# Twenty operand sums per second layer moved from VectorE to GpSimd, one unit ahead

## The chip, the cores and the metric

One core of one Trainium2 chip. The metric is the device time of one execution in microseconds (us). The engines are named as the profile names them: PE is TensorE's matmul, PEld its weight load, DVE is VectorE, ACT ScalarE, POOL GpSimd, SP the queue that issues the DMAs.

## The reference

```python
scores = scale * q @ k.T - log(S)          # 8 batches, 12 heads, 448 tokens, 64 per head
attn   = sigmoid(scores);  x = attn @ v    # x: 3584 tokens by 768
h = x @ w_in                               # 768 -> 2048
g = s * relu(h)**2 + b
out = g @ w_out                            # 2048 -> 768
```

All arrays are fp32, and products are taken nearly in fp32: an operand is split into a high part (its rounding to the format that TensorE multiplies) and a low part (the rest), and each product is three matmuls, high by high, high by low, low by high.

## The kernel before, in words

**Attention** (to 250 us of the span) writes x, transposed, to DRAM, while the weights are converted and their sums are made. **Tokens 0 to 511** pass through the feed-forward network in the plain way. The other six blocks of 512 tokens are done in two **threes**, n = 0 and 1, by a fast matrix algorithm with 15 products in place of 18. Each three has a first and a second layer.

In the **first layer** (the loop over L1, line 1080) the 15 products of x with w_in run in chains that add up in PSUM. Their results are combined on VectorE and ScalarE (`results_1`) into tiles G[m, h, p], with m the token block, h the half of the hidden dimension and p one of four parts. Each finished G is squared after its ReLU on VectorE (line 857) and scaled and shifted on ScalarE (line 860).

In the **second layer** (the loop over L2, line 1210) the 15 products come in the order 8, 13, 6, 10, 7, 1, 2, 3, 5, 4, 11, 12, 14, 0, 9, each with its four parts p: 60 **units** j of 12 matmuls. A unit's operand comes either straight from one G, from a G changed in place, or, for the products 6, 10, 7, 1 and 5, from a sum or difference of two G's in a fresh tile `gs_{n}_{i}_{p}`. 5 products by 4 parts are twenty fresh sums per second layer, forty in all.

`prep(j + LEAD)` with LEAD = 3, called behind unit j, makes the operand of the unit three ahead: its source (for the five products the sum, by `new`, line 1025), then its high part on ScalarE (`split_hi`, lines 678 and 680). The same call makes the low part of the unit two ahead on VectorE (`split_lo`, lines 181 and 689), and frees a fresh source. Two products also change G in place there: product 2 subtracts from G[0, 0], product 3 adds G[0, 0] to G[0, 1], which product 5's sums read later.

The order on each engine is the order in which the code is written; nothing reorders it. An engine runs ahead of the others as far as its waits let it. The tiles `gs`, `g_..h`, `g_..l`, `C` and others share 46 slots of one size (`heap`), handed out first freed, first used: a tile waits until the last reader of its slot's earlier tile is done. `results_2` copies the products' PSUM results out on ScalarE (line 1141) or combines them on VectorE with C tiles, and stores these. GpSimd has no work in this kernel beyond four constants at the start.

The weights `wu` come by DMA, one tile per unit, six units ahead.

Of the kernel before, what the change touches and what calls it, by code (L numbers as in the profile page):

```python
# [18 lines left out]
ALU = mybir.AluOpType  # L19
# [75 lines left out]
def sigmoid_attention_relu2_ffn(  # L95
# [10 lines left out]
    nc = tc.nc  # L106
    B, NQ, P, _, _, S = qk.shape
    D = v.shape[5]
    NF, _, DM = w_in.shape
# [67 lines left out]
    def add(o, x, y):  # L177
        nc.vector.tensor_tensor(o, x, y, op=ALU.add)  # L178

    def sub(o, x, y):  # L180
        nc.vector.tensor_tensor(o, x, y, op=ALU.subtract)  # L181
# [44 lines left out]
    def op(o, x, sign, y):  # L226
        (add if sign > 0 else sub)(o, x, y)
# [426 lines left out]
    L2 = [(i, p) for i in ORDER_2 for p in range(NPP)]  # L654
# [11 lines left out]
    def slot(name, r=False):  # L666
        return heap.tile([P, 2, TB], F32R if r else F32, name=name)
# [7 lines left out]
    def split_hi(raw, sign, name):  # L675
        hi = slot(name + "h", True)
        if sign > 0:
            nc.scalar.copy(hi, raw)
        else:
            nc.scalar.activation(hi, raw, AF.Copy, scale=-1.0)  # L680
        return hi

    def split_lo(raw, sign, hi, name, own):

        lo = slot(name + "l", True)
        if sign > 0:
            sub(lo, raw, f32(hi))
        else:
            nc.vector.scalar_tensor_tensor(
                lo, raw, -1.0, f32(hi), op0=ALU.mult, op1=ALU.subtract  # L690
            )
        if own:
            heap.free(raw)
        return lo
# [56 lines left out]
    def activate(f, ph):  # L751
        g = gp.tile([P, 2, TB], F32R, tag="g", name=f"g_{f}")
        r = rt.tile([P, TB], F32, tag="r", name=f"r_{f}")
        nc.scalar.activation(r, ph, AF.Relu)
        nc.scalar.activation(r, r, AF.Square)
        nc.scalar.activation(r, r, AF.Identity, bias=b_sb, scale=s_sb)
        nc.scalar.copy(g[:, 0], r)
        sub(g[:, 1], r, f32(g[:, 0]))
        return g
# [20 lines left out]
    for i, f in enumerate(order):  # L780
# [14 lines left out]
        g = activate(f, ph)  # L795
        if i + 1 < NF:
            w2[i + 1] = base(1, order[i + 1])
        j, stage = divmod(i - LATE_AT, LATE_FOR)
# [152 lines left out]
    for n, blocks in enumerate(threes):  # L951

        G = {}
# [6 lines left out]
        def results_1(i, p, bk):  # L960
# [9 lines left out]
            def final(m, h, neg=False):  # L970
                x = g(m, h)
                if (m, h) == (0, 0):
                    scales.append(lambda: (act_square(x), scale(x)))
                else:
                    later.append(lambda: (square(x, neg), scales.append(lambda: scale(x))))
# [36 lines left out]
            else:  # L1012
                add(g(2, 1), g(2, 1), bk)
                final(2, 1)

        def prep(j):

            if 0 <= j < len(L2):
                i, p = L2[j]
                own = True  # L1020

                def g(m, h):
                    return G[m, h, p]

                def new(x, sign, y):
                    t = slot(f"gs_{n}_{i}_{p}")
                    op(t, x, sign, y)
                    return t

                def drop(m, h):  # L1030
                    heap.free(G.pop((m, h, p)))

                def take(m, h):
                    return G.pop((m, h, p))

                if i in (8, 13, 2, 3):
                    src, own = G[{8: (1, 0), 13: (0, 1), 2: (2, 0), 3: (2, 1)}[i] + (p,)], False
                elif i == 6:
                    src = new(g(0, 1), -1, g(1, 0))
                elif i == 10:  # L1040
                    src = new(g(0, 1), 1, g(1, 1))
                elif i == 7:
                    src = new(g(0, 0), 1, g(1, 0))
                elif i == 1:
                    src = new(g(0, 0), 1, g(0, 1))
                elif i == 5:
                    src = new(g(2, 1), -1, g(0, 1))
                elif i == 4:
                    src = take(0, 1)
                elif i == 12:  # L1050
                    src = take(0, 0)
                elif i == 11:
                    add(g(1, 0), g(1, 0), g(1, 1))
                    src, own = G[1, 0, p], False
                elif i == 14:
                    sub(g(1, 0), g(2, 1), g(1, 0))
                    src, own = G[1, 0, p], False
                elif i == 0:
                    add(g(2, 0), g(2, 0), g(1, 0))
                    src = take(2, 0)  # L1060
                else:
                    sub(g(1, 1), g(2, 1), g(1, 1))
                    src = take(1, 1)
                sign = SECOND[i][1]
                gc[j] = (src, own, split_hi(src, sign, f"g_{n}_{i}_{p}"))
                if i == 2:
                    sub(g(0, 0), g(0, 0), g(2, 0))
                if i == 3:
                    add(g(0, 1), g(0, 1), g(0, 0))
                if i == 0:  # L1070
                    drop(1, 0)
                if i == 9:
                    drop(2, 1)
            j -= 1
            if 0 <= j < len(L2):
                i, p = L2[j]
                src, own, hi = gc[j]
                gc[j] = (hi, split_lo(src, SECOND[i][1], hi, f"g_{n}_{i}_{p}", own))

        for u, (i, p) in enumerate(L1):  # L1080
# [35 lines left out]
            if u >= len(L1) - LEAD:  # L1116
                prep(u - len(L1) + LEAD)
# [92 lines left out]
        for j, (i, p) in enumerate(L2):  # L1210
# [5 lines left out]
            g = gc.pop(j)  # L1216
            end = n + 1 == len(threes) and j + 1 == len(L2)

            for e, tk in LAST if end else [(e, slice(TB)) for e in range(KC)]:
# [11 lines left out]
                if end:  # L1231
                    x = C["t"][:, e, tk]
# [9 lines left out]
            if j in loads:  # L1242
                load_raw(n + 1, *loads[j])
            prep(j + LEAD)
            if later:
                later.popleft()()
# [43 lines left out]
```

## Time and profile before

| | us |
|---|---|
| median of 3 runs | 1038.89 |
| lowest and highest run | 1038.45, 1038.98 |
| the profiled execution, first to last instruction (span) | 1037.2 |
| first layer of three 0, on the chain of matmuls | 163.20 |
| second layer of three 0 | 163.20 |
| first layer of three 1 | 163.20 |
| second layer of three 1 | 163.28 |

The profiled execution's time is given by the page as its span alone; the median of the timed runs lies 1.7 us above it.

How to read the views. A row of the timeline has the start, the duration, the engine, the line, the operation, the tile written and the tiles read, and, in brackets, how long the engine had been idle before and who ended that. Buffer numbers are left out of the names: `g_2l` is the low part for part 2 of whichever product comes at that time, `gs` is a fresh sum, `h` and `o` are PSUM results of the first and the second layer. Line 178 is VectorE's add, line 181 its subtract; both are helpers, so the line alone doesn't tell the place. A row of groups has the count, the busy time and the mean of one, and the idle time before them.

### The profile page before, as it was taken

To read this page: it belongs to the slowest core of one execution; us is meant where nothing else is said; L and a number is where in the kernel's file an instruction comes from. 1 tells how busy PE (TensorE), PEld (TensorE's weight loads), DVE (VectorE), ACT (ScalarE), POOL (GpSimd) and SP (SyncE) were. 2 spreads that over 40 slices of the span, in tenths; PEclk is the share of its full clock that TensorE was granted. 3 is DMA by queue.
4 is the path that set the end of the run, shared out by engine and by line. 5 is a ranking of instruction groups with operands and counts; after the bars stand their busy time and mean duration, and the time that the engine had idled before them with its cause. 6 is when DMAs were issued, how large, how long until landed. Compare 5 with 4: busy or idle time off the path is not lost.

```text
span 1037.2 us, 13906 instructions
## 1 busy us (share of the span) xinstructions
PE 1033.5 (100%) x5290; PEld 780.9 (75%) x5290; DVE 837.3 (81%) x910; ACT 617.0 (59%) x666; POOL 0.2 (0%) x4
## 2 busy tenths in 40 slices
PE   9999999999999999999999999999999999999998
PEld 4545555555888888888888888888888888888887
DVE  5999999995988965898898897796455789888777
ACT  7999999988776755564445344344445335552432
POOL 0000000000000000000000000000000000000000
PEclk9999999999999999999999999999999999999999
DMA  9788989994999999999686676897666666676773
GB/s 334 265 333 340 359 321 393 345 398 190 338 362 366 358 409 410 340 341 322 201 267 190 218 230 219 292 317 249 197 192 194 194 192 196 191 233 212 221 227 119
DMA packets 101569, 287.17 MB, mean 277 GB/s; under 512 B 10240, under 2 KB 20352, under 8 KB 101504
## 3 DMA queue, kind: packets, MB, share of 16 engines
q1 hardware_dynamic: 101216, 285.84, 79.3%
q8 instruction: 42, 0.69, 0.3%
q10 hardware_dynamic: 288, 0.46, 0.1%
q14 instruction: 23, 0.19, 0.0%
HBM read 198.18 MB, written 88.08 MB: 276 GB/s over the span
## 4 chain that ended last, share of the span: by engine, by line
PE 100%; DVE 0%; issue 0%
PE o L1225 31%; PE h L1095 31%; PE pav L454 11%; PE psc L420 9%; PE ph L563 6%; PE po L765 6%; PE psc_l L441 2%; PE pav L463 2%; PE idle L482 0%; PE psc L426 0%; DVE C_t L181 0%
## 5 line engine op out<-in xcount | busy, mean ns | idle before, releaser
L1095 PE MATMUL h<-s_0h,wu 128*128 128x512 f32 x480 | 148.0, 389 | 0.0
L1095 PE MATMUL h<-s_1h,wu 128*128 128x512 f32 x480 | 147.8, 389 | 0.0
L400 ACT ACTIVATE a<-psc,nls 128x896 f32<-128x896 f32 x144 | 132.7, 1008 | 12.9 <-PE psc L420 10.1
L454 PE MATMUL pav<-a,v 128*64 128x448 f32 x576 | 113.8, 543 | 0.0
L1095 PEld LDWEIGHTS h<-s_0h,wu 128*128 128x128 f32 x480 | 90.1, 188 | 18.8
L1095 PEld LDWEIGHTS h<-s_1h,wu 128*128 128x128 f32 x480 | 90.1, 188 | 18.6
L968 ACT COPY G<-h 128x1024 f32<-128x1024 f32 x48 | 48.8, 1017 | 85.4 <-PE h L1095 57.7
L860 ACT ACTIVATE G<-G,b_sb,s_sb 128x1024 f32<-128x1024 f32 x48 | 59.8, 1246 | 61.4 <-DVE G L857 60.7
L1095 PE MATMUL h<-s_0l,wu 128*128 128x512 f32 x240 | 93.4, 389 | 0.0
L1095 PE MATMUL h<-s_1l,wu 128*128 128x512 f32 x240 | 93.4, 389 | 0.0
L454 PEld LDWEIGHTS pav<-a,v 128*64 128x64 f32 x576 | 39.1, 137 | 63.8 <-issue 45.4
L178 DVE TENSOR_TENSOR G<-G,h 128x1024 f32<-128x1024 f32 x40 | 48.8, 1219 | 39.1 <-PE h L1095 38.9
L1225 PE MATMUL o<-g_3h,wu 128*128 128x512 f32 (+1 forms) x244 | 79.0, 385 | 0.0
L1225 PE MATMUL o<-g_1h,wu 128*128 128x512 f32 x240 | 78.8, 389 | 0.0
L1225 PE MATMUL o<-g_2h,wu 128*128 128x512 f32 x240 | 78.8, 389 | 0.0
L1225 PE MATMUL o<-g_0h,wu 128*128 128x512 f32 x240 | 78.8, 389 | 0.0
L765 PE MATMUL po<-g,w 128*128 128x512 f32 x288 | 67.7, 389 | 0.0
L765 PEld LDWEIGHTS po<-g,w 128*128 128x128 f32 x288 | 54.1, 188 | 11.2
L563 PE MATMUL ph<-x0h,w 128*128 128x512 f32 x192 | 61.7, 390 | 0.0
L420 PE MATMUL psc<-qkh 64*128 64x448 f32 x284 | 54.8, 382 | 0.0
L1225 PEld LDWEIGHTS o<-g_3h,wu 128*128 128x128 f32 x244 | 45.6, 188 | 9.2
L1225 PEld LDWEIGHTS o<-g_0h,wu 128*128 128x128 f32 x240 | 45.1, 188 | 9.4
(152 smaller groups left out, 2029.7 us busy)
## 6 DMA issues: line engine op xcount, KB each, us to landing
wu<-wd SPq DMA_DIRECT2D x240, 512.0 KB, 3.8
wd<-t SPq DMA_DIRECT2D x36, 768.0 KB, 8.1
qk<-qk_t SPq DMA_DIRECT2D x23, 896.0 KB, 7.1
st<-w_out SPq DMA_DIRECT2D x16, 768.0 KB, 9.3
st<-w_in SPq DMA_DIRECT2D x16, 768.0 KB, 9.2
wd<-w SPq DMA_DIRECT2D x16, 768.0 KB, 5.9
v<-v_t SPq DMA_DIRECT2D x24, 448.0 KB, 5.4
xd<-xo SPq DMA_DIRECT2D x24, 448.0 KB, 4.4
```

The costliest lines, as they stand in the source:

```text
L178: nc.vector.tensor_tensor(o, x, y, op=ALU.add)
L400: nc.scalar.activation(a, psc[:, :, :S], AF.Sigmoid, bias=nls, scale=SCALE)
L420: nc.tensor.matmul(o[:, j, :S], two[wi][r, i, cols], two[xi][r, i, :S], start=m == 0, stop=m == 2,)
L441: nc.tensor.matmul(psc[half[i], j, :S], x[r, i, 1, 3 * P :], x[r, i, 0, :], start=True, stop=True,)
L454: nc.tensor.matmul(pav[r, i, :S], ld_[1][:, 3 * i + c, j, :], a[i, c][:, j, :], start=c == 0, stop=False,)
L463: nc.tensor.matmul(pav[r, i, :S], ld_[1][half[i], 6, j, :], a[half[i], j, :], start=False, stop=True,)
L563: nc.tensor.matmul(ph, w[:, k, wi, kc * P : (kc + 1) * P], x0[h][xi][:, cc, :], start=m == 0, stop=m == 3 * NCC - 1,)
L765: nc.tensor.matmul(pos[e], w[:, k, wi, kc * P : (kc + 1) * P], g[:, gi, :], start=first and i == 0, stop=last and i == 2,)
L860: nc.scalar.activation(x, x, AF.Identity, bias=b_sb, scale=s_sb)
L968: nc.scalar.copy(g(m, h), bk)
L1095: nc.tensor.matmul(bk[:, j], wt[:, j, wi, c * P : (c + 1) * P], opd[i][xi][:, c, :], start=i == ch[0] and m == 0, stop=m == 3 * KC - 1, sk ...
L1225: nc.tensor.matmul(o, wt[:, f, wi, e * P : (e + 1) * P], g[gi][:, f, tk], start=(end or i == ch[0] and p == 0) and f == 0 and m == 0, stop ...
```

## The change

The five kinds of sum move into a table. `prep(j)` first issues, on GpSimd, the sum for unit j + 1, if that unit is one of the five products, and keeps the tile in `made`; for unit j itself it takes the tile that the call before made. So a sum is issued one unit earlier than before, and on another engine.

```diff
+        NEW = {
+            6: ((0, 1), -1, (1, 0)), 10: ((0, 1), 1, (1, 1)), 7: ((0, 0), 1, (1, 0)),
+            1: ((0, 0), 1, (0, 1)), 5: ((2, 1), -1, (0, 1)),
+        }
+        made = {}
+
         def prep(j):
 
+            if 0 <= j + 1 < len(L2) and L2[j + 1][0] in NEW:
+                i, p = L2[j + 1]
+                x, sign, y = NEW[i]
+                made[j + 1] = slot(f"gs_{n}_{i}_{p}")
+                nc.gpsimd.tensor_tensor(
+                    made[j + 1], G[x + (p,)], G[y + (p,)], op=ALU.add if sign > 0 else ALU.subtract
+                )
...
-                def new(x, sign, y):
-                    t = slot(f"gs_{n}_{i}_{p}")
-                    op(t, x, sign, y)
-                    return t
...
-                elif i == 6:
-                    src = new(g(0, 1), -1, g(1, 0))
...
+                elif i in NEW:
+                    src = made.pop(j)
```

On VectorE, at the turn from product 13 to product 6 of three 0, stood before (gs_6_2 is the fresh sum for product 6, part 2; the number behind it is the buffer's):

```order
L181 TENSOR_TENSOR g_13_1l<-G_011_4114,g_13_1h 128x1024
L181 TENSOR_TENSOR g_13_2l<-G_012_4224,g_13_2h 128x1024
L181 TENSOR_TENSOR gs_6_0_5155<-G_010_4094,G_100_4355 128x1024
L181 TENSOR_TENSOR g_13_3l<-G_013_4243,g_13_3h 128x1024
L181 TENSOR_TENSOR gs_6_1_5175<-G_011_4114,G_101_4377 128x1024
L689 SCALAR_TENSOR_TENSOR g_6_0l<-gs_6_0_5155,g_6_0h 128x1024
L181 TENSOR_TENSOR gs_6_2_5195<-G_012_4224,G_102_4487 128x1024
```

and now, on the same engine:

```order
L181 TENSOR_TENSOR g_13_1l<-G_011_4114,g_13_1h 128x1024
L181 TENSOR_TENSOR g_13_2l<-G_012_4224,g_13_2h 128x1024
L181 TENSOR_TENSOR g_13_3l<-G_013_4243,g_13_3h 128x1024
L689 SCALAR_TENSOR_TENSOR g_6_0l<-gs_6_0_5137,g_6_0h 128x1024
L689 SCALAR_TENSOR_TENSOR g_6_1l<-gs_6_1_5157,g_6_1h 128x1024
L689 SCALAR_TENSOR_TENSOR g_6_2l<-gs_6_2_5177,g_6_2h 128x1024
```

The sums are gone from between the low halves, whose own order is as it was. They are GpSimd's queue now, whose first rows are these (it had no sums before; the first row is the branch at the program's start):

```order
L1286 UNCONDITIONAL_BRANCH
L1028 ISA
L1028 TENSOR_TENSOR gs_6_0_5137<-G_010_4094,G_100_4355 128x1024
L1028 TENSOR_TENSOR gs_6_1_5157<-G_011_4114,G_101_4377 128x1024
L1028 TENSOR_TENSOR gs_6_2_5177<-G_012_4224,G_102_4487 128x1024
L1028 TENSOR_TENSOR gs_6_3_5197<-G_013_4243,G_103_4505 128x1024
L1028 TENSOR_TENSOR gs_10_0_5219<-G_010_4094,G_110_4613 128x1024
```

GpSimd holds nothing but the forty sums, in the order of the units, so each starts when its two G's and its slot are there, whatever VectorE is at.

Later in the same layer, on VectorE, the low halves of product 3 (g_3) with the additions into G[0, 1] between them, before:

```order
L178 TENSOR_TENSOR G_013_4243<-G_013_4243,G_003_3946 128x1024
L689 SCALAR_TENSOR_TENSOR g_3_2l<-G_212_4139,g_3_2h 128x1024
L181 TENSOR_TENSOR gs_5_0_5645<-G_210_4007,G_010_4094 128x1024
L689 SCALAR_TENSOR_TENSOR g_3_3l<-G_213_4167,g_3_3h 128x1024
L181 TENSOR_TENSOR gs_5_1_5665<-G_211_4025,G_011_4114 128x1024
L181 TENSOR_TENSOR g_5_0l<-gs_5_0_5645,g_5_0h 128x1024
```

and now:

```order
L178 TENSOR_TENSOR G_013_4243<-G_013_4243,G_003_3946 128x1024
L689 SCALAR_TENSOR_TENSOR g_3_2l<-G_212_4139,g_3_2h 128x1024
L689 SCALAR_TENSOR_TENSOR g_3_3l<-G_213_4167,g_3_3h 128x1024
L181 TENSOR_TENSOR g_5_0l<-gs_5_0_5626,g_5_0h 128x1024
L181 TENSOR_TENSOR g_5_1l<-gs_5_1_5647,g_5_1h 128x1024
```

Product 5's sums no longer stand behind product 3's low halves; on GpSimd each waits only for the addition into its own G[0, 1, p]. On ScalarE and in SP's queue nothing changes its place.

More of the change, by code (lines that the diff above doesn't have):

```diff
@@ L1037, in prep @@
                     src, own = G[{8: (1, 0), 13: (0, 1), 2: (2, 0), 3: (2, 1)}[i] + (p,)], False
-                elif i == 6:
-                    src = new(g(0, 1), -1, g(1, 0))
[L1040 to L1047, printed above, removed]
+                elif i in NEW:
+                    src = made.pop(j)
                 elif i == 4:
```

## The prediction

> **What bounds the kernel now.** I read the page's busy times first, then the chain that ended last in order of time, then TensorE's waits.
>
> ```profile
> span 1037.2 us, 13906 instructions
> PE 1033.5 (100%) x5290; PEld 780.9 (75%) x5290; DVE 837.3 (81%) x910; ACT 617.0 (59%) x666; POOL 0.2 (0%) x4
> ```
>
> ```profile
> 544.55 163.20 PE o L1225 x720
> 707.75 163.20 PE h L1095 x720
> 870.95 163.28 PE o L1225 x726
> ```
>
> ```profile
> PE idle L482 <- PEq L1280: 0.8, 1, 0.8
> ```
>
> TensorE is busy for the whole span, the chain is matmuls almost throughout, and in all its waits there is one row, 0.8 us at the start. The two second layers take 163.20 us for 720 matmuls each: 226.7 ns per matmul, 2.72 us per unit of 12. So VectorE's relief can't shorten the chain: work taken off an engine that nobody on the chain waits for is worth nothing. What the change can do is make an operand late. The question is how late VectorE's low halves run against the matmul that reads them.
>
> The timeline of TensorE gives the due times, the second layer's first two matmuls on the high and the low tile of product 8, part 0:
>
> ```profile
> 544.39 0.39 PE L1225 MATMUL o<-g_0h,wu 128*128 128x512 f32 x1
> 544.62 0.39 PE L1225 MATMUL o<-g_0l,wu 128*128 128x512 f32 x1
> ```
>
> So the low tile of unit j is due at 544.62 + 2.72 j. The timeline of VectorE around that point:
>
> ```profile
> 522.83 1.22 DVE L181 TENSOR_TENSOR G<-G,h 128x1024 f32<-128x1024 f32 x1 [0.24 <-PE h L1095]
> 524.08 1.22 DVE L857 SCALAR_TENSOR_TENSOR G<-G 128x1024 f32<-128x1024 f32 x1
> 525.55 1.22 DVE L181 TENSOR_TENSOR G<-G,h 128x1024 f32<-128x1024 f32 x1 [0.24 <-PE h L1095]
> 526.80 1.22 DVE L857 SCALAR_TENSOR_TENSOR G<-G 128x1024 f32<-128x1024 f32 x1
> 528.27 1.22 DVE L181 TENSOR_TENSOR G<-G,h 128x1024 f32<-128x1024 f32 x1 [0.24 <-PE h L1095]
> ...
> 539.15 1.22 DVE L181 TENSOR_TENSOR G<-G,h 128x1024 f32<-128x1024 f32 x1 [0.24 <-PE h L1095]
> ...
> 543.69 1.22 DVE L181 TENSOR_TENSOR g_1l<-G,g_1h 128x1024 fp32r<-128x1024 f32 x1
> 544.82 1.22 DVE L857 SCALAR_TENSOR_TENSOR G<-G 128x1024 f32<-128x1024 f32 x1
> 545.96 1.21 DVE L178 TENSOR_TENSOR G<-G,h 128x1024 f32<-128x1024 f32 x1
> 547.21 1.22 DVE L857 SCALAR_TENSOR_TENSOR G<-G 128x1024 f32<-128x1024 f32 x1
> 548.35 1.22 DVE L181 TENSOR_TENSOR g_2l<-G,g_2h 128x1024 fp32r<-128x1024 f32 x1
> 550.68 1.23 DVE L181 TENSOR_TENSOR g_3l<-G,g_3h 128x1024 fp32r<-128x1024 f32 x1 [1.12 <-ACT g_3h L678]
> ```
>
> The low tile of product 8, part 2, ends at 548.35 + 1.22 = 549.57 and is due at 544.62 + 5.44 = 550.06: 0.49 us of slack, at the turn from first to second layer, with VectorE dense. This is the place to watch.
>
> **The change part by part.** What it removes, from the groups kept apart by shape, with the rows that I use as prices:
>
> ```profile
> L178 DVE TENSOR_TENSOR gs<-G,G 128x1024 f32<-128x1024 f32 x24 | 29.2, 1219 | 0.0
> L181 DVE TENSOR_TENSOR gs<-G,G 128x1024 f32<-128x1024 f32 x16 | 19.5, 1219 | 0.0
> L1280 POOL MEMSET const-bfloat16-1.0<- 128x1 bf16 x1 | 0.1, 101 | 0.0
> L164 DVE MEMSET nls<- 128x1 f32 x1 | 0.1, 59 | 0.8 <-PEq L1280 0.8
> L860 ACT ACTIVATE G<-G,b_sb,s_sb 128x1024 f32<-128x1024 f32 x48 | 59.8, 1246 | 61.4 <-DVE G L857 60.7
> L211 DVE TENSOR_SCALAR st<-st 128x768 int32<-128x768 int32 x32 | 18.0, 564 | 1.1
> L208 DVE SCALAR_TENSOR_TENSOR wf<-st,wf 128x768 int32<-128x768 int32 x32 | 30.4, 950 | 0.0
> ```
>
> *Removed:* 24 + 16 sums, 48.7 us of VectorE. Beside a TensorE that doesn't wait: 0.
>
> *Added:* 40 sums on GpSimd. No row shows one. Below: no faster than VectorE, 1.22 us. Above: two whole passes of the slowest elementwise row of this size, 2 x 1.246 = 2.49 us. The only operation that both engines run is a MEMSET of one column, 101 against 59 ns; 1.219 x 101 / 59 = 2.09 us, an estimate, is the value I take.
>
> *GpSimd's own pace.* Its queue holds nothing else, so its waits hold up nobody's other work. A sum's slot is one freed earlier. In both threes the third sum (product 6, part 2) takes a slot that TensorE's last first-layer matmuls read, free at 544.4; the fourth's is free after unit 0, and from product 7 on each slot after the unit eight before. By 2.09 us against 2.72 it stays far ahead. The last of the 14 sums of that run (product 1, part 3, unit 23) must be done two conversions before 544.62 + 23 x 2.72 = 607.18, at 607.18 - 1.22 - 1.05 = 604.9 (1.05 us is ScalarE's high conversion, in a row below), so only a sum over (604.9 - 544.4) / 14 = 4.3 us would be late by itself. Cost 0.
>
> *The new waits.* ScalarE's high conversion now waits for GpSimd; behind it in its queue stand the PSUM copies of line 1141 and the next conversions, VectorE's low half waits for it, TensorE for both. At the pace above these waits are over before they begin. SP's queue keeps its order: 0.
>
> ```profile
> 601.38 1.05 ACT L678 CAST g_3h<-gs 128x1024 fp32r<-128x1024 f32 x1
> ```
>
> *The unknown: do the two engines hinder each other?* No row has them side by side. The bounds of what one GpSimd sum costs VectorE are 0 and its whole 2.09 us. The nearest rows are the last two of the groups: 564 ns with one input, 950 ns with two, at the same 768 elements. A two-input operation on SBUF thus uses all the read width that VectorE has; I take that it finds none beside a GpSimd sum, so the two exclude each other, first come first served. An operation with one input in PSUM (h, o) I let run beside. Then, by hand, VectorE's operations 1.14 us apart (547.21 to 548.35):
>
> (1) The turn. The first sum's slot is a stored weight tile's, free at its landing:
>
> ```profile
> L902 SPq DMA_DIRECT2D wd<-t_p x2: 319/372/424, 519.3 to 519.6; - x2
> DMA to landing us min/median/max: 2.9/3.0/3.2
> ```
>
> 519.6 + 3.2 = 522.8. Sums one and two run 522.8 to 524.9 and 526.05 to 528.15; the squares at 524.08 and 526.80 slip, the second by 1.35 us. Five gaps of 0.24 us (528.27 to 539.15, one per unit) take that back to 0.15. Sum three comes at 544.4 and gets in when the running low half ends, 545.0 to 547.1; the square runs 547.1 to 548.24; sum four 548.24 to 550.34, beside the PSUM operation; the next square starts at 550.34 rather than 547.21, and the low tile ends at 550.34 + 1.14 + 1.22 = 552.70, due at 550.06. **2.64 us.**
>
> (2) The run of 16 units. One sum and one low half take 2.09 + 1.14 = 3.23 us, 0.51 more than a unit. The low tile of product 6, part 0, is ended at 564.97 in this replay, due at 544.62 + 21.76 + 2.64 = 569.02: 4.05 ahead. Eleven rounds to product 7, part 3, lose 5.6, one round where the sum's slot isn't free yet gives 2.09 back. 0.5 left: **0.** By 2.49 us: about 3.7 ahead, eleven times 0.91, 2.49 back: 3.8 late.
>
> (3) Product 5. Its sums read tiles that VectorE updates two units earlier:
>
> ```profile
> 609.87 1.23 DVE L181 TENSOR_TENSOR C<-o,C 128x1024 f32<-128x1024 f32 x1 [0.57 <-PE o L1225]
> ...
> 613.28 1.22 DVE L178 TENSOR_TENSOR G<-G,G 128x1024 f32<-128x1024 f32 x1
> 614.41 1.22 DVE L181 TENSOR_TENSOR g_3l<-G,g_3h 128x1024 fp32r<-128x1024 f32 x1
> 615.55 1.22 DVE L178 TENSOR_TENSOR G<-G,G 128x1024 f32<-128x1024 f32 x1
> ...
> 621.22 1.22 DVE L689 SCALAR_TENSOR_TENSOR g_2l<-G,g_2h 128x1024 fp32r<-128x1024 f32 x1
> ```
>
> Each update frees one sum, which then holds up the next two operations: sums at 615.55, 619.92, 624.29 and 628.66. The low tiles of product 3, parts 1, 2 and 3, end at 624.37, 628.74 and 631.97, due (unit 29 on) at 623.50, 626.22 and 628.94: 0.87, then 1.65 more, then 0.51 more. **3.03 us.** At 609.87 VectorE restarts from a wait on TensorE, so what (1) cost has moved both engines alike, and (1) and (3) add.
>
> Sum per three 2.64 + 0 + 3.03 = 5.67; the second three's rows lie 326.40 us later (544.55 to 870.95) in the same pattern, so 11.3 in all. The profiled span becomes 1037.2 + 11.3 = 1048.5; the median of the runs is 1.7 above the span, so **1050.2 us**. By a sum of 2.49 us: (1) 4.1, (2) 3.8, (3) 4.6, twice 12.5, or 1063.9. By 0 hindrance: 1038.9.
>
> The Trainium skill, "SBUF — State Buffer", section "Who interferes with whom", says that a VectorE instruction with two SBUF inputs contends with a GpSimd instruction that reads SBUF, and that whichever starts first holds the shared port for its whole length; that speaks against this change, and no run here shows it yet. By that rule the sum is the one above, by none it is 1038.9. Its page "GPSIMD Engine Reference", section "Performance versus the Vector engine", times the same add at 4497 ns on GpSimd and 2293 on VectorE; an estimate from it, 1.219 x 1.96 = 2.39 us, would put the same sum at about 1060.
>
> **The rivals.** *It costs nothing* (not slower): the two engines read without hindrance, or VectorE keeps its right of way. For it: GpSimd's sums run up to seven units early, and VectorE gets back 1.14 us per unit. Against it: the 0.49 us of slack, and the ratio of 564 to 950. Place and point: the turn, where 2.09 us of hindrance per sum make 2.64 + 0.49 = 3.13 us; at x us per sum 1.5 x - 0.49, which stays under 1.04 per three up to x = 1.0; place (3) is late only from 4 x = 8.36 - 3.03, x = 1.3. So up to half of the full hindrance the time is within 0.2%: 1038.9.
>
> *GpSimd is too slow by itself:* at 5 us a sum, without hindrance, the run ends 14 x 5 - 60.5 = 9.5 us late per three, 19 in all, 1058. For it: POOL has never run such an operation here. Against it: 101 ns beside 59.
>
> *It gets faster:* nothing on the chain waits for VectorE; no mechanism, 2%.
>
> **How the numbers follow.** 0.2%, 2.1 us, is about what a measurement of this kernel can tell from no change. By the bounds alone the point x = 1.0 halves the span from 0 to 2.09; the two-input row tips it to hindrance. Forecast 0.65, all slower; GpSimd's own pace 0.05, slower; no cost 0.28, same; faster 0.02. The range must reach the no-cost case, so it starts at the lowest run, 1038.4; it ends at 1064, the sum by 2.49 us. The forecast's own range is 1041 to 1064.
>
> **What would show it.** Right: two-input VectorE rows (L857, low halves) longer than 1.22 us, or gaps in front of them, wherever POOL is busy, and PSUM rows at 1.22; TensorE waits on g tiles, first at product 8, part 2 or 3, then at product 3; second layers over 163.2 us by some 5.7, first layers unchanged. POOL rows near 2.1 us. Wrong: all VectorE rows at 1.22 beside a busy POOL and no TensorE wait; or TensorE waiting for GpSimd's sums through ScalarE, in the run of 16 units, with VectorE idle.

## The result and the profile after

| | before | after |
|---|---|---|
| median, us | 1038.91 (4 runs) | 1055.81 (4 runs) |
| lowest and highest run | 1038.45, 1038.98 | 1054.9, 1056.42 |
| span of the profiled execution | 1037.2 | 1053.4 |

The ratio is 1.0162, with a 95% interval from 1.0149 to 1.0174: slower by 16.9 us, where 11.3 were forecast. The page's first lines after the change:

```profile
span 1053.4 us, 13982 instructions
PE 1038.4 (99%) x5290; PEld 780.8 (74%) x5290; DVE 867.8 (82%) x870; ACT 615.0 (58%) x666; POOL 126.1 (12%) x44
```

VectorE has 40 instructions fewer, and its busy time has still gone up, from 837.3 to 867.8 us. TensorE, which waited for nothing in the middle of the kernel before, now has these rows ahead of the 0.8 us at the start in its waits (us in total, times, longest):

```profile
PE o L1225 <- DVE g_2l L181: 5.1, 2, 2.6
PE o L1225 <- DVE g_2l L689: 2.9, 2, 1.4
PE o L1225 <- DVE g_1l L689: 2.0, 2, 1.0
PE o L1225 <- DVE g_3l L689: 1.1, 4, 0.3
```

All are waits for a low tile of the second layer, none for GpSimd or ScalarE (a short wait of the weight loads in the first layer is told further down). TensorE's timeline in three 0 shows where three of them end; the first is at the turn (product 8, part 2), the second and third at product 3, parts 1 and 2:

```profile
553.35 0.80 PE L1225 MATMUL o<-g_2l,wu 128*128 128x512 f32 x1 [2.55 <-DVE g_2l L181]
...
629.91 0.50 PE L1225 MATMUL o<-g_1l,wu 128*128 128x512 f32 x1 [0.98 <-DVE g_1l L689]
634.39 0.50 PE L1225 MATMUL o<-g_2l,wu 128*128 128x512 f32 x1 [1.44 <-DVE g_2l L689]
```

VectorE at the turn, beside GpSimd's queue (its x2 row is two sums back to back, 5.81 us in all):

```profile
545.41 3.42 DVE L857 SCALAR_TENSOR_TENSOR G<-G 128x1024 f32<-128x1024 f32 x1
548.75 1.21 DVE L178 TENSOR_TENSOR G<-G,h 128x1024 f32<-128x1024 f32 x1
549.99 2.17 DVE L857 SCALAR_TENSOR_TENSOR G<-G 128x1024 f32<-128x1024 f32 x1
552.09 1.21 DVE L181 TENSOR_TENSOR g_2l<-G,g_2h 128x1024 fp32r<-128x1024 f32 x1
```

```profile
523.21 5.75 POOL L1028 TENSOR_TENSOR gs<-G,G 128x1024 f32<-128x1024 f32 x2 [522.77 <-DMA wd<-t_p]
545.27 5.81 POOL L1028 TENSOR_TENSOR gs<-G,G 128x1024 f32<-128x1024 f32 x2 [16.32 <-ACT G L860]
```

The square at 545.41 starts behind a sum that started at 545.27. It took 1.22 us before and takes 3.42 now, 2.20 more. The add at 548.75 reads one operand from PSUM (h), runs beside the second sum, and takes 1.21. The square at 549.99 is held for the rest of that sum. In the run of 16 units the two engines take turns. VectorE's timeline there:

```profile
587.92 3.41 DVE L689 SCALAR_TENSOR_TENSOR g_0l<-gs,g_0h 128x1024 fp32r<-128x1024 f32 x1
591.26 3.42 DVE L689 SCALAR_TENSOR_TENSOR g_1l<-gs,g_1h 128x1024 fp32r<-128x1024 f32 x1
```

One round (one sum, one low half) takes 591.26 - 587.92 = 3.34 us, against 2.72 us per unit of TensorE. Before product 5 the updates of G and the low tiles of product 3 alternate, and each update is held:

```profile
625.29 3.43 DVE L178 TENSOR_TENSOR G<-G,G 128x1024 f32<-128x1024 f32 x1
628.64 1.21 DVE L689 SCALAR_TENSOR_TENSOR g_1l<-G,g_1h 128x1024 fp32r<-128x1024 f32 x1
629.78 3.42 DVE L178 TENSOR_TENSOR G<-G,G 128x1024 f32<-128x1024 f32 x1
```

The whole loss can be laid out along TensorE. I compared the start of each of the matmuls in the two traces, one by one, and noted where the lag against the kernel before grows (us):

| place | three 0 | three 1 |
|---|---|---|
| ahead of the first three's first layer (in attention, at 6.94 us) | 0.12 | |
| first layer, product 14, part 1 | 0.42 | 0 |
| turn, product 8, part 2: the wait | 2.71 | 2.71 |
| the matmuls right behind it | 1.46 | 0.11 |
| product 7, parts 2 and 3 (end of the run) | 0.45 | 0.64 |
| product 3, part 1 | 1.25 | 1.26 |
| product 3, part 2 | 1.71 | 1.68 |
| product 3, part 3 | 0.58 | 0.58 |

That is 15.7 of the 16.2 us by which the span grew; the rest is in steps of about 0.02 us or less. The 0.12 us lie ahead of every instruction that the change touches, so they belong to this execution and not to the change. The first matmul after each of the waits is 0.11 us longer before the next one starts (0.34 against 0.23 us); this is in the rows of products 7 and 3, and is the 0.11 behind the turn in three 1. The 1.46 in three 0 is another thing. In windows of 5 us around that wait TensorE's granted clock (the last column but two) falls:

```profile
550.00:555.00 5.00, 2.45 (x8) 1.70 (x7) 3.89 (x3) 2.91 (x4) 1.08 (x1) 0.79 0.49 167
555.00:560.00 5.00, 5.00 (x21) 4.07 (x20) 5.00 (x4) 2.22 (x3) 2.67 (x1) 0.87 0.30 78
```

The loss is 5 x (0.21 + 0.13) = 1.7 us of clock, which is half clock for 3.4 us; the matmuls in it start 0.43 us apart instead of 0.23. In the trace the half clock lasts from 552.85 to 556.27 us: it sets in 0.5 us before the wait ends, and the 2.92 us behind the wait cost TensorE half of that, the 1.46. The same wait in three 1 has no such stretch; the last section shows why (window of TensorE alone, granted clock again the last but two):

```profile
885.00:890.00 5.00, 2.45 (x11) 1.00 0.43 139
```

### The profile page after: what moved, and what is told of

Read it like the earlier page. It is cut to its first block, busy times and chain, and to the rows that moved or that the text cites. A ratio compares the mean times of both kernels' runs of the same rounds, so it can differ in the third digit from the quotient of the medians.

```text
span 1053.4 us, 13982 instructions
## 1 busy us (share of the span) xinstructions
PE 1038.4 (99%) x5290; PEld 780.8 (74%) x5290; DVE 867.8 (82%) x870; ACT 615.0 (58%) x666; POOL 126.1 (12%) x44
## 4 chain that ended last, share of the span: by engine, by line
PE 85%; DVE 12%; issue 3%; DVEq 0%
PE h L1095 29%; PE o L1225 20%; PE pav L454 11%; PE psc L420 9%; PE ph L563 6%; PE po L765 6%; DVE G L178 2%; PE psc_l L441 2%; PE pav L463 2%; DVE g_2l L689 2%; DVE G L857 2%; DVE g_1l L689 2%; DVE g_3l L689 1%; DVE g_0l L689 1%; DVE G L181 1%
## 5 line engine op out<-in xcount | busy, mean ns | idle before, releaser
L1028 POOL TENSOR_TENSOR gs<-G,G 128x1024 f32<-128x1024 f32 x40 | 125.9, 3168 | 843.9 <-DMA wd<-t_p 522.8
L857 DVE SCALAR_TENSOR_TENSOR G<-G 128x1024 f32<-128x1024 f32 x40 | 58.3, 1458 | 1.0
L1225 PE MATMUL o<-g_2l,wu 128*128 128x512 f32 x120 | 47.9, 399 | 8.0 <-DVE g_2l L181 5.1
```

Of the source, the lines that this page charges most:

```text
L857: nc.vector.scalar_tensor_tensor(x, x, 0.0, x, op0=ALU.min if neg else ALU.max, op1=ALU.mult)
L1028: nc.gpsimd.tensor_tensor(made[j + 1], G[x + (p,)], G[y + (p,)], op=ALU.add if sign > 0 else ALU.subtract)
L1225: nc.tensor.matmul(o, wt[:, f, wi, e * P : (e + 1) * P], g[gi][:, f, tk], start=(end or i == ch[0] and p == 0) and f == 0 and m == 0, stop ...
```

## The experiments

The theory: a GpSimd sum and a VectorE instruction that reads its operands from SBUF exclude each other, so each sum costs VectorE up to its own length, and TensorE waits where VectorE's low tile had less slack than that. The main rivals: the unit ahead in the order does the harm; the slots or the additional tile do it; GpSimd's sums are simply too slow.

### Only a part of the sums on GpSimd

Three kernels move only some of the products. The condition decides which; the other sums are made by VectorE, at the place they had before. (The code cuts of the experiments are against the changed kernel, if nothing else is said, and `...` stands for lines that are left out.)

```diff
-            if 0 <= j + 1 < len(L2) and L2[j + 1][0] in NEW:
+            if 0 <= j + 1 < len(L2) and L2[j + 1][0] in (6, 10, 7, 1):   # or (5,), or (10,)
...
```

All but product 5:

> Product 5's eight sums are back on VectorE, the other 32 stay on GpSimd. Theory (a GpSimd sum and a VectorE operation with two SBUF inputs exclude each other): the waits at product 3 go, 1.25 + 1.71 + 0.58 = 3.5 us per three in the changed kernel's matmul starts, the others stay: 1055.8 - 7.1 = 1048.7 us. Rival (each GpSimd sum costs TensorE the same, 16.9 us over 40): 1055.8 - 8 x 0.42 = 1052.4 us.

Measured: 1047.77 us, ratio 1.009 (1.0075 to 1.0105). TensorE's waits at product 3 are gone, those at the turn (g_2l, line 181) and at the end of the run (g_3l, product 7) stay:

```profile
PE o L1230 <- DVE g_2l L181: 5.1, 2, 2.6
...
PE o L1230 <- DVE g_3l L689: 0.5, 2, 0.3
```

Product 5 alone:

> Only product 5's eight sums are on GpSimd. Theory: the waits at product 3 alone, 1038.9 + 7.1 = 1046 us, with nothing at the turn and nothing at product 7. Rival (the same cost per sum): 1038.9 + 8 x 0.42 = 1042.3 us. If the two parts add up, this loss and that of the kernel without product 5 together are 16.9 us.

Measured: 1046.3 us, ratio 1.0072 (1.0059 to 1.0086). The complement shows:

```profile
PE o L1230 <- DVE g_2l L689: 2.9, 2, 1.5
PE o L1230 <- DVE g_1l L689: 2.0, 2, 1.0
...
PE o L1230 <- DVE g_3l L689: 0.6, 2, 0.3
```

Against the runs of the kernel before, 1038.61 us on that chip, the two lose 9.2 and 7.7 us, together 16.9, which is the whole change. So places (1) and (3) add, and the loss sits where the replay had put it.

Product 10 alone:

> Only product 10's eight sums are on GpSimd, where VectorE's low tiles are 5 us ahead of TensorE in the kernel before. Theory: VectorE rows of 3.4 us beside these sums, but 4 x 2.2 us of hindrance less 4 x 1.14 us of relief is 4.2 us, inside the slack: 1039 us, within 0.6 of the kernel before. Rival (the same cost per sum): 1042.3 us.

Measured: 1043.33 us, ratio 1.0044 (1.0032 to 1.0057). My expectation failed here. I had thought that product 10, in the middle of the run, has slack enough. GpSimd's and VectorE's timelines show why it hasn't:

```profile
557.78 6.02 POOL L1028 TENSOR_TENSOR gs<-G,G 128x1024 f32<-128x1024 f32 x2 [2.93 <-PE o L1230]
566.10 3.32 POOL L1028 TENSOR_TENSOR gs<-G,G 128x1024 f32<-128x1024 f32 x1 [2.30 <-DVE g_0l L689]
```

```profile
558.13 3.43 DVE L181 TENSOR_TENSOR g_3l<-G,g_3h 128x1024 fp32r<-128x1024 f32 x1
...
567.08 3.42 DVE L689 SCALAR_TENSOR_TENSOR g_1l<-gs,g_1h 128x1024 fp32r<-128x1024 f32 x1
```

GpSimd has an empty queue and starts a sum as soon as its slot and its inputs allow: the four of three 0 at 552.34, 557.78, 560.43 and 566.10 us, where VectorE started them at 565.42, 569.49, 571.76 and 574.03 in the kernel before, so three to five units (of 2.72 us) early. The low tiles that it holds there are those of products 13 and 6, and TensorE's wait of 1.46 us, in front of the matmul on product 6, part 1, at 570.56, follows the row at 567.08. (The other three has the same wait, of 1.42 us.) VectorE's relief, the sums of product 10 that it no longer makes, comes only behind that. What a moved instruction costs is to be looked for where it runs, not where its result is due.

### The unit ahead

All sums stay on VectorE, but are issued a unit ahead as in the change:

```diff
-                nc.gpsimd.tensor_tensor(
-                    made[j + 1], G[x + (p,)], G[y + (p,)], op=ALU.add if sign > 0 else ALU.subtract
-                )
+                op(made[j + 1], G[x + (p,)], sign, G[y + (p,)])
```

> All forty sums stay on VectorE but are issued one unit ahead, as the change issues them. Theory: the order alone costs nothing, 1038.9 us. Rival (the earlier slots, and the low tiles behind a sum at the turn, are what makes TensorE wait): 2 us or more above the kernel before.

Measured: 1039.34 us, ratio 1.0005 (0.9997 to 1.0014), and no wait of TensorE but the 0.8 us at the start. The order alone costs nothing that can be measured. The other half, GpSimd's sums at the place where the kernel before issues them (against the kernel before):

```diff
 def new(x, sign, y):
     t = slot(f"gs_{n}_{i}_{p}")
-    op(t, x, sign, y)
+    nc.gpsimd.tensor_tensor(t, x, y, op=ALU.add if sign > 0 else ALU.subtract)
     return t
```

> The sums are made by GpSimd as in the change, but are issued where the kernel before has them, not a unit ahead. Theory (the sums collide with VectorE's low tiles wherever they run): the waits at the turn and at product 3 stay, about 1053 to 1057 us. Rival (issuing them a unit ahead is what hurts): near 1039 to 1042 us.

Measured: 1056.27 us, ratio 1.0168 (1.0153 to 1.0183), the same as the change within the intervals. The distribution differs. Its second sum, still in the first layer, and its third, at the turn, then one of its waits at the turn and two of five in the run of three 0, from the timelines:

```profile
538.52 2.42 POOL L1027 TENSOR_TENSOR gs<-G,G 128x1024 f32<-128x1024 f32 x1 [13.69 <-PE h L1095]
546.86 2.41 POOL L1027 TENSOR_TENSOR gs<-G,G 128x1024 f32<-128x1024 f32 x1 [5.91 <-PE o L1225]
```

```profile
551.53 0.50 PE L1225 MATMUL o<-g_2l,wu 128*128 128x512 f32 x1 [1.81 <-DVE g_2l L181]
587.37 0.50 PE L1225 MATMUL o<-g_3l,wu 128*128 128x512 f32 x1 [0.18 <-DVE g_3l L689]
590.71 0.50 PE L1225 MATMUL o<-g_0l,wu 128*128 128x512 f32 x1 [0.28 <-DVE g_0l L689]
```

With one sum at the turn instead of two, that wait is shorter by 0.7 us in each three; but the sums start later, and at 3.34 us per round the run of 16 units loses 2.8 and 2.7 us by the comparison of starts, where the change loses 0.45 and 0.64. Issuing ahead is thus a help in the run and a harm at the turn.

### Work for GpSimd beside an unchanged VectorE

In the next three kernels all sums stay on VectorE, and GpSimd does something in addition at each of the 40 places, into a tile that nobody reads. They differ by what GpSimd reads:

```diff
+                t = slot(f"gx_{n}_{i}_{p}")
+                nc.gpsimd.memset(t, 0.0)                 # or tensor_copy(t, G[x + (p,)])
+                heap.free(t)                             # or the sum itself, into t
...
```

Nothing (a fill):

> All sums on VectorE as before; in addition GpSimd fills a tile of the same size with a constant wherever the change has a sum: it writes SBUF and reads none. Theory (what collides is the reading): VectorE rows at 1.22 us beside busy GpSimd, 1038.9 us. Rival (any GpSimd instruction on SBUF holds VectorE up): VectorE rows longer than 1.22 us by a fill's length, TensorE waits at the turn, over 1041 us.

Measured: 1038.84 us, ratio 0.9998 (0.9989 to 1.0007). GpSimd writes for 38 us, VectorE's low halves keep their 1.22 us, and TensorE waits for none of them:

```profile
L1028 POOL MEMSET gx<- 128x1024 f32 x40 | 38.0, 957 | 906.5 <-DMA wd<-t_p 522.2 <-PE h L1099 244.6 <-PE o L1229 56.1
```

Neither the slots, nor the waits that an instruction on GpSimd brings, nor its writes cost anything. One operand (a copy):

> All sums stay on VectorE, as in the kernel before, and GpSimd in addition copies one of the two tiles G into a tile that nobody reads, once per sum (one SBUF operand read instead of two). Theory (what stands in VectorE's way is any GpSimd instruction that reads SBUF): the VectorE instructions with two SBUF inputs grow from 1.22 us by up to the length of a copy, about 1 to 1.5 us, on the same 40 occasions, and the kernel takes 1042 to 1050 us, less than the 1090.6 us of the additional sums. Rival (only GpSimd's two-input sums stand in the way): rows stay at 1.22 us, 1038.9 us.

Measured: 1041.96 us, ratio 1.0031 (1.0019 to 1.0042), just under the 1042 to 1050 us that the theory expected. VectorE's low halves are held; its PSUM rows and those that find GpSimd idle are not. VectorE's timeline, and then GpSimd's copies, the last of them alone:

```profile
587.68 1.21 DVE L178 TENSOR_TENSOR gs<-G,G 128x1024 f32<-128x1024 f32 x1
588.81 2.06 DVE L689 SCALAR_TENSOR_TENSOR g_1l<-gs,g_1h 128x1024 fp32r<-128x1024 f32 x1
590.79 1.21 DVE L181 TENSOR_TENSOR C<-C,o 128x1024 f32<-128x1024 f32 x1
```

```profile
587.88 1.91 POOL L1028 COPY gx<-G 128x1024 f32<-128x1024 f32 x1 [1.20 <-DVE g_0l L689]
591.00 1.04 POOL L1028 COPY gx<-G 128x1024 f32<-128x1024 f32 x1 [1.20 <-PE o L1229]
```

A copy takes 1.04 us and costs a VectorE row 2.06 - 1.21 = 0.85. Two operands (the sum):

> All sums on VectorE as before; in addition GpSimd makes the same sums into a tile that nobody reads, so nobody waits for GpSimd's results. Theory: each of the forty holds VectorE up by 2.2 us, with no relief: per three 16 x 2.2 = 35 us less some 10 us of idle time and slack, and 6 us at product 3, so about 60 us in all, 1085 to 1105 us. Rival (TensorE's waits come from waiting for GpSimd's results): 1039 us.

Measured: 1090.6 us, ratio 1.0496 (1.0477 to 1.0516). VectorE's rows of two SBUF inputs are mostly at 1.21 or 3.42, as in the change:

```profile
590.04 3.31 POOL L1028 TENSOR_TENSOR gx<-G,G 128x1024 f32<-128x1024 f32 x1 [1.16 <-DVE g_0l L689]
```

```profile
589.88 1.21 DVE L178 TENSOR_TENSOR gs<-G,G 128x1024 f32<-128x1024 f32 x1
591.01 3.42 DVE L689 SCALAR_TENSOR_TENSOR g_1l<-gs,g_1h 128x1024 fp32r<-128x1024 f32 x1
```

Fill, copy and sum, or none, one and two operands read, hold VectorE by 0, 0.85 and 2.20 us. What collides is GpSimd's reading. These 51.7 us (1090.6 - 1038.9) are also what GpSimd's sums cost when VectorE isn't relieved of any, four stretches of half clock included. The change pays 16.9: the relief, worth nothing by itself, makes up for most of the hindrance.

### Halves

Each sum is made by two instructions of 512 columns:

```diff
+                for c in range(2):
                     nc.gpsimd.tensor_tensor(
-                        made[j + 1], G[x + (p,)], G[y + (p,)], ...
+                        made[j + 1][:, c], G[x + (p,)][:, c], G[y + (p,)][:, c], ...
```

> Each GpSimd sum is issued as two of half the columns. Theory (held for a whole instruction, first come first served): VectorE rows beside GpSimd shrink from 3.42 to about 2.4 us; a low tile and a half take 2.3 us, less than a unit, so product 7's wait goes, the turn costs about 2.5 us and product 3 3.5 us per three: about 1051 us. Rival (the two engines share read width in proportion, at any length of instruction): rows of 3.4 us stay and so does the time, 1056 us.

Measured: 1052.21 us, ratio 1.0127 (1.0112 to 1.0141). One of VectorE's low halves in the run:

```profile
585.70 2.32 DVE L689 SCALAR_TENSOR_TENSOR g_0l<-gs,g_0h 128x1024 fp32r<-128x1024 f32 x1
```

One instruction is held for half a sum, 2.32 - 1.22 = 1.10 us. So the lock lies on single instructions, not on a whole queue, and whoever has waited gets in between two of them. There is no wait at product 7 any more, but the turn is as late as before (2.68 us of idle TensorE): there it is the sum of the sums' lengths that counts.

### Low halves with one input

Do only VectorE instructions with two SBUF inputs collide? In the change, the low tiles of the second layer are made by a copy from one SBUF tile; the low part is thereby left out of the result.

```diff
+        if name[0] == "g":
+            nc.vector.tensor_copy(lo, raw)
-        if sign > 0:
+        elif sign > 0:
             sub(lo, raw, f32(hi))
```

> The change as it is, but the low half tiles of the second layer are made by a copy with one input instead of the subtraction with two; the low part is left out of the result by that. Theory (only VectorE instructions with two SBUF inputs are held by a GpSimd sum): the copies run at about 0.7 us beside GpSimd, only the few other two-input instructions are held, and the time is 1046 to 1049 us or less. Rival (a one-input VectorE instruction on SBUF is held as well): rows of about 2.9 us beside GpSimd, and 1051 to 1056 us.

The profiled execution took 1042.96 us, the only other one 2699.11, without a trace. I ran the kernel again, and beside it the one with such copies and all sums on VectorE:

> The kernel with copies for the second layer's low halves and the sums on GpSimd once more, unchanged: one of its two executions took 2699 us without a trace, the profiled one 1042.96 us. Theory (the long one was a disturbance that has nothing to do with this kernel): 1042 to 1044 us in all executions, the copies that start while a sum runs at 2.9 us. Rival (the kernel has a second way of running): again some executions far longer.

> As the run with copies for the second layer's low halves (the low part is left out of the result again), but with the sums on VectorE: GpSimd idle. Theory (the 4.1 us lost there are all hindrance by GpSimd's sums, held copies among them): no waits of TensorE for a low tile, copies all at 0.69 us, 1038.9 us. Rival (the copies themselves or their order cost): about 1041 to 1043 us.

Measured: 1043.25 us (1042.74 to 1043.32 in five executions), ratio 1.0039 (1.0025 to 1.0054); and 1038.67 us with the sums on VectorE, ratio 0.9998 (0.9987 to 1.0008), no waits. The long execution didn't come back; what it was stays open. VectorE just behind the turn in the repeated kernel, and GpSimd:

```profile
551.44 0.68 DVE L687 CAST g_3l<-G 128x1024 fp32r<-128x1024 f32 x1
...
554.45 2.88 DVE L687 CAST g_0l<-gs 128x1024 fp32r<-128x1024 f32 x1
```

```profile
554.27 2.51 POOL L1030 TENSOR_TENSOR gs<-G,G 128x1024 f32<-128x1024 f32 x1 [3.31 <-PE o L1227]
```

A copy takes 0.68 us when GpSimd is idle (551.44) and 2.88 when a sum has just started (554.45, behind the sum of 554.27): held by the same 2.20 us as a two-input instruction. So my narrower theory, that one input escapes, fell: this copy, which alone takes 0.68 us where a two-input instruction takes 1.22, is held as well. The rival's size was wrong too, since shorter copies leave VectorE more slack: 1043 and not 1051 to 1056. Only the rows with an operand in PSUM stay free.

## Why the prediction held, and where its sizes were off

**TensorE never waits, so the relief shortens nothing** held: no kernel was measurably faster than the one before. For the same reason I have no version to offer that beats it.

**GpSimd's sum**: estimated 2.09 us, measured 2.42 and 2.41 when alone (the two rows at 538.52 and 546.86). So the ratio of two MEMSETs of one column was a poor guide. What the replay needs is not the sum's length, though, but for how long it holds VectorE, and that is 2.20 us, 0.11 more than the 2.09. That the two are so close is luck: with 2.41 as the hold, the prediction's own two results (1050.2 us at 2.09, 1063.9 at 2.49) would have given about 1061, an estimate. The page "GPSIMD Engine Reference" of the Trainium skill, section "Performance versus the Vector engine", gave an estimate of 2.39 by its ratio, and the trace agrees. Its own pace cost 0, as forecast: no wait for POOL appears on TensorE.

**The assumption that carries the forecast**, exclusion first come, first served, PSUM operations beside it, is shown by the held rows of 3.42, by GpSimd's own rows where VectorE came first (3.31 at 590.04 with additional sums), by the 1.21 of the PSUM rows and by the three additional works. The Trainium skill, "SBUF — State Buffer", section "Who interferes with whom", has this rule: the shared port is held for a whole instruction, GpSimd instructions that only write don't contend with VectorE's two-input ones, and copies in a two-port mode can contend; the traces agree with the first two, with 2.20 and 0 us, and the copy was held by 2.20 us, but in which mode it ran no trace shows.

**(1) The turn**: 2.64 forecast, 2.71 measured. That these are so close is luck, because two errors met here. The low tile ended 0.60 us later than in the replay (552.09 + 1.21 = 553.30, not 552.70): the sums were longer, and the third started at 545.27 rather than 545.0. And TensorE was late itself, by 0.54 us: by the 0.12 from attention, and by 0.42 from a wait in the first layer, which moved the due time. That wait is a term that the prediction lacks ("first layers unchanged"). VectorE after the change, squares held by the first two sums, and TensorE's weight load:

```profile
524.20 2.49 DVE L857 SCALAR_TENSOR_TENSOR G<-G 128x1024 f32<-128x1024 f32 x1
526.61 1.21 DVE L181 TENSOR_TENSOR G<-G,h 128x1024 f32<-128x1024 f32 x1
527.85 2.18 DVE L857 SCALAR_TENSOR_TENSOR G<-G 128x1024 f32<-128x1024 f32 x1
```

```profile
531.22 0.19 PEld L1095 LDWEIGHTS h<-s_0h,wu 128*128 128x128 f32 x1 [0.57 <-DVE G L181]
```

The subtract that starts when the second square ends (529.96) reads product 6's h out of PSUM, and product 14, which adds to the same h, waits until it has been read. The kernel whose sums are not issued ahead has one sum there and the second only at 538.52, and it has no such wait. The low tiles were not the only due times; VectorE's reading of PSUM results has them too.

**(2) The run of 16 units**: 0 forecast, 0.45 and 0.64 us measured. A round takes 3.34 us, not 3.23, and eleven rounds use up 1.2 us more, where the replay had 0.5 left. Mis-sized by the hold of 2.20 us.

**(3) Product 5's sums**: 3.03 forecast, 3.54 and 3.52 measured. Of the difference 0.33 is the 0.11 us that each of three waits costs TensorE on top of its length; the rest, under 0.2, fits the longer hold.

**Not in the prediction at all**: half clock at the first turn, 1.35 us beyond the usual 0.11.

So the forecast of +11.3 us lacked 5.6: about 1.0 from (3), 1.1 from (2), 0.1 from (1), 0.2 from the restarts behind the two turns, 1.35 from the clock, 0.4 from the first layer, 0.1 before the first three's first layer. The small steps add 0.5. The last 0.7 come from the median, which lies 2.4 us above the profiled span, against 1.7 before: the profiled execution took 1055.26 us, 0.55 less than the median. The two longer ones of the four (1056.42 and 1056.36) list a granted clock of 0.997 instead of 0.998. A second stretch of half clock, 1.7 us of clock in 1053, would make that difference, but they left no trace. Together that is some 5.5 of the 5.6. The rivals fell: no cost by the held rows and the 16.9 us, GpSimd's own pace by the absence of a wait for it.

## What to carry to other kernels

Work that is moved from VectorE to GpSimd is not off VectorE as long as GpSimd reads SBUF and VectorE's instructions take all their operands from there too: here a sum of 2.41 us on GpSimd held VectorE for up to 2.20, more than the 1.22 us that it saved. Before such a move, list the slack of each tile that VectorE makes, for its consumers and for the PSUM results that it must read, around the time when the moved instruction will really start, which on an idle engine is as early as its inputs and its slot allow. If TensorE waits for nothing, there is nothing to gain from relief in the first place.

## What the runs showed of the hardware

**Half clock around short waits.** The granted clock fell to half for 3.4 us at some waits of TensorE: at 2.55 us in the change (three 0, not three 1), at 2.56 us with product 5's sums on VectorE (three 1, not three 0), at 2.68 us with halves (three 0, not three 1), and at waits of 3.77 and about 2.8 us with additional sums in all four cases. In the traces it never did at a wait of 1.9 us or less. Two windows of the run with additional sums, around the wait of 3.77:

```profile
550.00:555.00 5.00, 1.37 (x7) 1.00 0.59 192
555.00:560.00 5.00, 4.86 (x15) 0.66 0.00 0
```

5 x 0.34 = 1.7 us of clock, as in the change.

Why one of two equal waits brings half clock and the other doesn't can be read from the same traces. The clock changes on a grid. In the change it was first full at 6.72 us and fell at 552.85, which is 160 times 3.413 us later; in the other three kernels the falls come 161 (halves), 257 (without product 5) and 161, 168, 264 and 271 (additional sums) such steps after the first full clock. The grid's start differs from run to run (3.46 to 6.72 us), so it doesn't follow the kernel. What counts is how long TensorE is idle within one of these stretches of 3.413 us:

| kernel, three | wait, us | most idle time in one stretch, us | clock in the next stretch |
|---|---|---|---|
| change, three 0 | 2.55 | 2.05 | 0.5 |
| change, three 1 | 2.55 | 1.81 | 1.0 |
| without product 5, three 0 | 2.56 | 1.35 | 1.0 |
| without product 5, three 1 | 2.56 | 2.46 | 0.5 |
| halves, three 0 | 2.68 | 2.37 | 0.5 |
| halves, three 1 | 2.68 | 1.85 | 1.0 |
| additional sums, wait at the turn, both threes | 3.77 | 3.41 | 0.5 |
| additional sums, the next wait, both threes | 2.80 | 2.80 | 0.5 |

Over all the traces, before the last matmuls, every stretch with 2.05 us of idle time or more was followed by half clock, and none with 1.85 us or less. Whether a wait of 2.55 us brings half clock is therefore chance: it depends on how the grid cuts it. Where the limit lies between 1.85 and 2.05 us stays open: two executions of the kernel that issues nothing ahead list a clock of 0.998, the other two 1.0, so its waits of 1.81 and 1.87 us may be enough when the grid leaves one whole, but the two left no trace.

The Trainium skill, "TensorE: Matmul & The Clock Gate", section "Part 1: The HAM clock gate", has half clock after an idle window of about 3.4 us, in windows that run freely. The grid and its varying start agree with that; that 2.05 us of idle time in a window were enough does not agree with a wholly idle one.

**Restarts.** Every wait for a low tile at full clock delayed the matmul that waited by 0.16 us more than the idle time shown (2.71 for 2.55, 1.15 for 0.98), since a matmul's row is 0.39 us long where the next one usually starts after 0.23. It cost another 0.11 us in that first matmul itself.
